# Other forms for the unread products ahead of the first head's maxima

## The chip, the cores and the metric

The kernel runs on one core of one Trainium2 chip. The metric is the time of one execution in device microseconds (us); the kernel before takes 967.83 us, the median of three runs (967.53 to 968.13).

## What is computed

Attention with a hash mask for 4 x 8 heads of 768 positions and 64 dimensions, and then a two-layer network on its result:

```python
q_bucket = np.sum(((q @ proj) > 0) * powers, -1)   # 6 bits; k_bucket likewise
scores = where(q_bucket[..., None] == k_bucket[..., None, :], scale * q @ k.T, -1e9)
attn = exp(scores - max(scores)); attn = attn / (sum(attn) + 1e-9)
x = (attn @ v) as [3072, 512]
h = x @ w_in                                        # 512 -> 2048
g = where(h >= 1, h, where(h <= -1, 0, (h + 1)**2 / 4))
return g @ w_out                                    # 2048 -> 512
```

## The kernel before, in words

All is float32. Where float32 accuracy is needed from single-pass products, an operand is split into a high part, rounded to the type float32r ("split form"), and the rest. The 32 heads are worked off in units of 128 keys x 384 queries: two products make the scores (lines 421 and 422), ScalarE takes the exponential, and three products gather the values (lines 454, 456, 458). The row maxima of a head are computed a few heads ahead by products of their own (line 343) that VectorE reduces (line 350). The network runs after that and between. Instructions of an engine run in the order in which the program writes them; a table of tasks per unit sets that order from the first unit on, and plain statements set it before.

The change touches only the start, which is written out by hand for pair 0:

- `keep_busy` (line 475) is one product whose result nobody reads. It multiplies `idle`, a 128 x 256 tile of zeros in float32r, by its first 128 columns, into a scratch half of a PSUM bank. It stands in four places: 14 times at the start, 5 times after the first head's bit products, once after each of the six score products of `max_first`, and 4 times later into another bank.
- `first_mm` (line 238) makes the hash bits of a head from two products for each half of the positions; ScalarE copies part of it (line 242), VectorE compares (line 247), and ScalarE and VectorE write the scaled bits (lines 254 and 256) into the tile that the score products read.
- `max_first` (line 495) computes the first half of the first head's maxima: six score products of 384 columns, each with an unread product after it and a VectorE maximum (line 498). Four PSUM tiles are taken in turn.
- After that come the second head's bit products (line 238 again), the next two score products (line 343), whose maxima VectorE takes at line 350, and three small products that turn the maxima into a row (line 274).
- `max_tr` (line 396) is the one place before where a float32 transposition runs on TensorE; line 398 does the same in split form as a product with the identity.

The order of the start is:

Of the kernel before, what the change touches and what calls it, by code (L numbers as in the profile page):

```python
# [11 lines left out]
F32 = mybir.dt.float32  # L12
# [8 lines left out]
B, H, S, D = 4, 8, 768, 64  # L21
NB = 6
P = 128
# [88 lines left out]
def attention(ctx, tc, wst, T1, T2, qk, v, pj, cv, x_d, s_d, e_d, tasks, shared):  # L112
    nc = tc.nc
# [10 lines left out]
    def half_bank(hf):  # L124
        return ps_f.tile([P, 512], F32, name=f"half{hf}")
# [8 lines left out]
    ident = const.tile([P, P], F32, name="ident")  # L134
# [3 lines left out]
    idle = const.tile([P, 2 * P], F32R, name="idle")  # L138
# [60 lines left out]
    def ones_row(h, eng):  # L199
        eng.memset(T2[0][32:33, 1, h].bitcast(F32), 1.0)  # L200
# [43 lines left out]
    def first_cmp(h, hf):  # L244
        sl = slice(hf * HS, (hf + 1) * HS)
        neg = neg_first[h]
        nc.vector.tensor_tensor(out=neg[:, sl], in0=neg_first[h, hf][0:40, 0:HS], in1=neg[:, sl], op=ALU.is_gt)
# [70 lines left out]
    def first_half(hd, a, b):  # L318
        return obank[1][:, 448 + hd * NJ + a:448 + hd * NJ + b] if in_bank(hd, a) else nmp(hd)[:, a:b]
# [6 lines left out]
    def nmp(hd):  # L326

        if hd not in nms:
            nms[hd] = small.tile([P, 2 * NJ], F32, name="nm")
        return nms[hd]  # L330
# [139 lines left out]

    scratch = half_bank(0)

    def keep_busy(ps=scratch):

        nc.tensor.matmul(out=ps[:, 0:2 * P], lhsT=idle[:, 0:P], rhs=idle, start=True, stop=True)  # L475

    def weights_pair(part):

# [9 lines left out]
    def max_first():  # L488

        t2 = T2[0]  # L490
        nm = first_half(0, 0, NJ), nmp(0)[:, NJ:2 * NJ]
        for hf in range(2):
            for i in range(NJ // 2):
                sm = ps_s.tile([P, 512], F32, name="s")
                nc.tensor.matmul(out=sm[:, 0:HS], lhsT=t2[:, 0, 0, i * P:(i + 1) * P],
                                 rhs=t2[:, 1, 0, hf * HS:(hf + 1) * HS], start=True, stop=True)
                keep_busy()
                nc.vector.tensor_reduce(out=nm[hf][:, i:i + 1], in_=sm[:, 0:HS], axis=AX.X,
                                        op=ALU.max, negate=True)

# [25 lines left out]
    nc.vector.memset(idle.bitcast(F32), 0.0)  # L526
    nc.vector.memset(pw.bitcast(F32), 0.0)
    nc.vector.memset(T2[0][0:64, 0].bitcast(F32), 0.0)
    for _ in range(14):
        keep_busy()  # L530
    make_identity(nc, ident)
    nc.gpsimd.tensor_copy(out=ident_r, in_=ident)
    for t in nrow:
# [15 lines left out]
    for hf in range(2):  # L549
        first_mm(0, hf, obank[hf])  # L550
    ones_row(0, nc.gpsimd)
    for _ in range(5):
        keep_busy()
    first_cmp(0, 0)
    first_scale(0, 0, nc.vector, 0)
    first_scale(0, 1, nc.scalar, 0)
# [5 lines left out]
    prep_first(1, first[1][:, 0], nc.gpsimd)  # L562
    place_first(1)
    max_first()
    row_clamp(0, 0, NJ // 2)
    for hf in range(2):
# [104 lines left out]
    for i in range(2 * NJ):  # L671
        n = 5 * 31 + 35 * i // 4
# [497 lines left out]
def lsh_attn_ffn(ctx: ExitStack, tc: tile.TileContext, qk, v, pj, cv, w_in, w_out, out):  # L1170
# [105 lines left out]
    for i in (2, 3):  # L1276
        at(NH * NU + 2 * i - 10, late[i + NFT - NW1][0])
    attention(actx, tc, wst, T1, T2, qk, v, pj, cv, x_d, s_d, e_d, tasks, attn)
    actx.close()

# [78 lines left out]
```

## Time and profile before

| what | us |
|---|---|
| median of the runs | 967.83 |
| the profiled execution: span from the first to the last instruction | 965.5 |
| what lies around the span, by the median | 2.3 |
| TensorE (PE) busy in the span | 957.1 |
| VectorE (DVE), ScalarE (ACT), GpSimd (POOL) busy | 752.7, 679.8, 322.7 |

The profiled execution has no time of its own beside its span. An engine's time is how long at least one of its instructions was on it; products are pipelined, so the duration of one is longer than its step to the next, and what a row of several tells is the distance of the starts. PEld is the loading of weights, which runs beside the product before it.

### The profile page before, as it was taken

The page shows a single profiled execution, that of the slowest core. Times are in us where ns is not written, and L with a number is a line of the kernel's source. Part 1 is how long each engine was busy: PE and PEld are TensorE (multiplying, and loading weights), DVE is VectorE, ACT ScalarE, POOL GpSimd, SP SyncE. Part 2 cuts the span into 40 slices and gives each one's busy share as a digit, 9 for nine tenths or more (in the row PEclk, how much of TensorE's full clock was granted, in tenths as well). Part 3 has the DMA queues.
Part 4 walks back from the last instruction along what each step waited for, and adds up shares of the span by engine and source line. Part 5 has one row for each costly group of instructions (what it writes and reads, how often), then busy time and mean ns, then how long its engine had stood idle before and what let it go on. Part 6 is the DMA issues. An engine that isn't in the chain of part 4 may idle for free.

```text
span 965.5 us, 15605 instructions
## 1 busy us (share of the span) xinstructions
PE 957.1 (99%) x5050; PEld 889.9 (92%) x5050; DVE 752.7 (78%) x1341; ACT 679.8 (70%) x1481; POOL 322.7 (33%) x435
## 2 busy tenths in 40 slices
PE   8999999999999999999999999999999999999998
PEld 7899999999999999999989998888998899888996
DVE  8878889888888889885987787787866777655554
ACT  7889999999999999987655465555564545544444
POOL 8867776666667776476000000000000000000000
PEclk9999999999999999999999999999999999999999
DMA  5776666666766666536691669966468554454431
GB/s 163 189 178 181 164 169 174 183 180 198 202 180 188 158 174 167 148 107 170 186 344 44 200 214 310 308 216 184 120 186 215 156 175 120 147 150 119 121 88 65
DMA packets 95112, 167.55 MB, mean 174 GB/s; under 512 B 13956, under 2 KB 51960, under 8 KB 95032
## 3 DMA queue, kind: packets, MB, share of 16 engines
q1 hardware_dynamic: 94768, 166.53, 60.1%
q8 instruction: 40, 0.66, 0.3%
q14 instruction: 40, 0.33, 0.1%
q10 hardware_dynamic: 264, 0.03, 0.0%
HBM read 106.13 MB, written 33.87 MB: 145 GB/s over the span
## 4 chain that ended last, share of the span: by engine, by line
PE 97%; DVE 2%; ACT 1%; issue 0%; DVEq 0%
PE y L893 27%; PE h L1125 18%; PE h L1030 7%; PE s L421 7%; PE o L458 7%; PE o L456 7%; PE o L454 7%; PE s L422 7%; PE smax L343 6%; PE o L219 2%; PE half L343 1%; DVE nm L350 0%; PE half L475 0%; DVE nm L323 0%; PE s L398 0%
## 5 line engine op out<-in xcount | busy, mean ns | idle before, releaser
L430 ACT ACTIVATE ph<-s 128x384 fp32r<-128x384 f32 x380 | 189.8, 500 | 32.1 <-PE s L422 26.1
L360 DVE TENSOR_REDUCE nm<-smax 128x1 f32<-128x768 f32 x168 | 159.9, 952 | 17.5 <-PE smax L343 17.5
L39 DVE TENSOR_TENSOR pl<-s,ph 128x384 fp32r<-128x384 f32 x256 | 137.9, 550 | 26.9 <-ACT s L435 25.6
L39 POOL TENSOR_TENSOR pl<-pf,ph 128x384 fp32r<-128x384 f32 x128 | 129.8, 1014 | 84.3 <-ACT pf L435 79.4
L858 DVE SCALAR_TENSOR_TENSOR t<-t 128x384 f32<-128x384 f32 x128 | 71.3, 557 | 106.7 <-ACT z L853 106.5
L421 PE MATMUL s<-t 128*128 128x384 f32 x384 | 130.5, 340 | 0.0
L454 PE MATMUL o<-ph,va 128*128 128x386 f32 x384 | 130.0, 339 | 0.0
L456 PE MATMUL o<-ph,vb 128*128 128x386 f32 x384 | 130.0, 338 | 0.0
L458 PE MATMUL o<-pl,va 128*128 128x386 f32 x384 | 130.0, 338 | 0.0
L422 PE MATMUL s<-t 128*128 128x384 f32 x384 | 129.4, 337 | 0.0
L435 ACT ACTIVATE s<-s 128x384 f32<-128x384 f32 x252 | 126.2, 501 | 0.0
L893 PE MATMUL y<-t,ghi 128*128 128x512 f32 x384 | 124.6, 395 | 0.0
L852 ACT ACTIVATE t<-h,mh 128x384 f32<-128x384 f32 x56 | 32.5, 581 | 83.7 <-PE h L1030 44.1
L343 PE MATMUL smax<-t 128*128 128x384 f32 x336 | 87.6, 342 | 0.4 <-DVE nm L360 0.3
L863 ACT CAST ghi<-z 128x384 fp32r<-128x384 f32 x129 | 65.2, 505 | 30.1 <-DVE z L859 26.3
L853 ACT ACTIVATE z<-t,m 128x384 f32<-128x384 f32 x128 | 79.0, 617 | 4.2
L893 PEld LDWEIGHTS y<-t,ghi 128*128 128x128 f32 x384 | 71.3, 188 | 11.0 <-ACT ghi L863 0.3
L1125 PE MATMUL h<-wbig,t 128*128 128x384 f32 x399 | 81.4, 336 | 0.0
L852 ACT ACTIVATE t<-wsq,mh 128x384 f32<-128x384 f32 x48 | 29.6, 617 | 67.0 <-DVE wsq L1138 40.8
L1125 PEld LDWEIGHTS h<-wbig,t 128*128 128x128 f32 x399 | 71.6, 188 | 5.2
L893 PE MATMUL y<-t,glo 128*128 128x512 f32 x192 | 76.0, 396 | 0.0
L893 PE MATMUL y<-woh,glo 128*128 128x512 f32 x192 | 75.7, 394 | 0.2
(206 smaller groups left out, 2104.2 us busy)
## 6 DMA issues: line engine op xcount, KB each, us to landing
t<-wc SPq DMA_DIRECT2D x92, 256.0 KB
t<-t SPq DMA_DIRECT2D x60, 384.0 KB
wraw<-wc SPq DMA_DIRECT2D x76, 256.0 KB
raw<-in_qk_dram SPq DMA_DIRECT2D x14, 768.0 KB
wraw<-in_w_in_dram SPq DMA_DIRECT2D x16, 512.0 KB
wraw<-in_w_out_dram SPq DMA_DIRECT2D x16, 512.0 KB
t<-ed SPq DMA_DIRECT2D x36, 192.0 KB
xd<-xs SPq DMA_DIRECT2D x32, 192.5 KB
```

Of the source, the lines that this page charges most:

```text
L39: eng.tensor_tensor(out=out, in0=a, in1=b, op=ALU.subtract)
L343: nc.tensor.matmul(out=ps[:, 0:HS], lhsT=t2[:, 0, h, i * P:(i + 1) * P], rhs=t2[:, 1, h, hf * HS:(hf + 1) * HS], start=True, stop=True)
L360: nc.vector.tensor_reduce(out=nmp(hd)[:, i:i + 1], in_=smax[hd][:, :, 0:HS], axis=AX.XY, op=ALU.max, negate=True)
L421: nc.tensor.matmul(out=ps[:, 0:HS], lhsT=t1[:, 1, h, ks], rhs=t1[:, 0, h, sl], start=True, stop=False)
L422: nc.tensor.matmul(out=ps[:, 0:HS], lhsT=t2[:, 1, h, ks], rhs=t2[:, 0, h, sl], start=False, stop=True)
L430: nc.scalar.activation(out=ph[:, 0:HS], in_=ps[:, 0:HS], func=AF.Exp, scale=SCALE)
L435: nc.scalar.activation(out=pf, in_=ps[:, 0:HS], func=AF.Exp, scale=SCALE)
L454: nc.tensor.matmul(out=o, lhsT=wa, rhs=ph, start=(jj == 0), stop=False)
L456: nc.tensor.matmul(out=o, lhsT=wb, rhs=ph, start=False, stop=False)
L458: nc.tensor.matmul(out=o, lhsT=wa, rhs=pl, start=False, stop=(jj == NJ - 1))
L893: nc.tensor.matmul(out=ys[c][m], lhsT=g_[:, m * P:(m + 1) * P], rhs=w, start=(first and k == 0), stop=(last and k == 2))
L1125: nc.tensor.matmul(out=ps, lhsT=w[:, cs], rhs=x, start=(n == 0 and s not in (2, 3, 6)), stop=(n == 5), skip_group_check=True)
```

## The change

`keep_busy` gets a form and a count. Form 0 is the old product. Form 1 is a plain float32 product of 66 columns, form 2 a split-form product of 130 columns, form 3 a split-form product of 66 columns, and the last is a float32 transposition of 128 columns. The weights have 128 columns in every form, taken from the first and second half of `idle` in turn. Results are unread as before.

```diff
+    idle_f = idle.bitcast(F32)
+
+    def keep_busy(ps=scratch, form=0, n=1):
+
+        for i in range(n):
+            ks = slice(i % 2 * P, (i % 2 + 1) * P)
+            if form == 0:
+                nc.tensor.matmul(out=ps[:, 0:2 * P], lhsT=idle[:, 0:P], rhs=idle, start=True, stop=True)
+            elif form == 1:
+                nc.tensor.matmul(out=ps[:, 0:D + 2], lhsT=idle_f[:, ks], rhs=idle_f[:, 0:D + 2], start=True, stop=True)
+            elif form == 2:
+                nc.tensor.matmul(out=ps[:, 0:P + 2], lhsT=idle[:, ks], rhs=idle[:, 0:P + 2], start=True, stop=True)
+            elif form == 3:
+                nc.tensor.matmul(out=ps[:, 0:D + 2], lhsT=idle[:, ks], rhs=idle[:, 0:D + 2], start=True, stop=True)
+            else:
+                nc.tensor.transpose(out=ps[:, 0:P], in_=idle_f[:, ks], identity=ident)
...
-                keep_busy()
+                keep_busy(form=(0, 1, 2, 3, 4, 1)[hf * 3 + i], n=(1, 3, 4, 4, 3, 3)[hf * 3 + i])
...
-    for _ in range(14):
-        keep_busy()
+    for form, n in ((0, 2), (1, 5), (2, 4), (3, 4), (0, 3)):
+        keep_busy(form=form, n=n)
...
-    for _ in range(5):
-        keep_busy()
+    for form, n in ((0, 2), (1, 4), (2, 4), (3, 2)):
+        keep_busy(form=form, n=n)
```

On TensorE, at the start of the program: the first set, ahead of the first head's four bit products (into the tiles `o_137` and `o_138`); `half_169` is the scratch.

```order
-L475 MATMUL half_169<-idle 128x256 x14
+L480 MATMUL half_169<-idle 128x256 x2
+L482 MATMUL half_169<-idle 128x66 x5
+L484 MATMUL half_169<-idle 128x130 x4
+L486 MATMUL half_169<-idle 128x66 x4
+L480 MATMUL half_169<-idle 128x256 x3
 L238 MATMUL o_137<-t_0_77,pw 128x384
```

Fourteen calls have become eighteen, five of them plain float (L482); the bit products follow as before.

On TensorE, from the second set to the second head's bit products, in the changed program (the six `L508` products are the first head's scores):

```order
L480 MATMUL half_169<-idle 128x256 x2
L482 MATMUL half_169<-idle 128x66 x4
L484 MATMUL half_169<-idle 128x130 x4
L486 MATMUL half_169<-idle 128x66 x2
L508 MATMUL s<-t_0_77 128x384
L480 MATMUL half_169<-idle 128x256
L508 MATMUL s<-t_0_77 128x384
L482 MATMUL half_169<-idle 128x66 x3
L508 MATMUL s<-t_0_77 128x384
L484 MATMUL half_169<-idle 128x130 x4
L508 MATMUL s<-t_0_77 128x384
L486 MATMUL half_169<-idle 128x66 x4
```

Before, five wide products stood ahead of the first score and one after each; now there are twelve, and then one, three, four and four.

On TensorE, the end of that stretch in the changed program:

```order
L508 MATMUL s<-t_0_77 128x384
L488 MATMUL half_169<-ident,idle 128x128 x3
L508 MATMUL s<-t_0_77 128x384
L482 MATMUL half_169<-idle 128x66 x3
L238 MATMUL s<-t_0_77,pw 128x384
```

Three transpositions and three plain-float products stand where one wide product stood each time, ahead of the second head's bit products. The rows count calls. The built program holds 5088 products and 5088 weight loads where the one before holds 5050 of each; 23 calls were added, so the 15 plain-float calls (5, 4, 3 and 3) make up the other 15, as two loads and two products each. VectorE, ScalarE, GpSimd and the DMA queues keep their instructions and their order.

## Rows read from the trace of the kernel before

**Rows 1.** The page: the span, the first engine's busy time, share and count, and the chain that ended last by engine.

```profile
span 965.5 us, 15605 instructions
PE 957.1 (99%) x5050; PEld 889.9 (92%) x5050; DVE 752.7 (78%) x1341; ACT 679.8 (70%) x1481; POOL 322.7 (33%) x435
PE 97%; DVE 2%; ACT 1%; issue 0%; DVEq 0%
```

**Rows 2.** Busy time by stretch: the stretch, its length, busy us and instructions of each engine, the granted TensorE clock, the DMA share and GB/s.

```profile
0.00:20.00 20.00, 17.13 (x85) 14.33 (x86) 17.39 (x42) 15.15 (x32) 15.53 (x48) 1.00 0.59 168
20.00:40.00 20.00, 19.16 (x105) 16.71 (x104) 17.04 (x37) 16.20 (x39) 18.59 (x26) 1.00 0.62 156
40.00:60.00 20.00, 19.13 (x101) 16.87 (x100) 17.48 (x34) 15.82 (x37) 14.33 (x20) 1.00 0.63 165
60.00:80.00 20.00, 20.00 (x115) 19.58 (x114) 16.65 (x26) 17.51 (x43) 12.28 (x16) 1.00 0.74 194
```

**Rows 3.** The chain of work that ended last, in order of time, in the first 13 us: start, us, what.

```profile
1.27 3.36 PE half L475 x14
4.63 1.66 PE o L238 x4
...
6.82 0.71 ACT t L254
...
8.79 0.57 DVE o L498
...
10.01 1.40 DVE nm L498 x3
```

**Rows 4.** TensorE in order of time from the first unread product to the score products at line 343: start, us to the end of the last of the row, line, output and inputs, count, and the wait before with its releaser.

```profile
1.27 3.36 PE L475 MATMUL half<-idle 128*128 128x256 f32 x14 [1.27 <-DVE idle L526]
4.57 1.70 PE L238 MATMUL o<-t,pw 128*128 128x384 f32 x4
6.07 0.81 PE L475 MATMUL half<-idle 128*128 128x256 f32 x5
7.66 0.41 PE L495 MATMUL s<-t 128*128 128x384 f32 x1 [0.78 <-ACT t L254]
...
8.02 0.34 PE L495 MATMUL s<-t 128*128 128x384 f32 x1
8.20 0.28 PE L475 MATMUL half<-idle 128*128 128x256 f32 x1
8.32 0.34 PE L495 MATMUL s<-t 128*128 128x384 f32 x1
...
8.77 0.44 PE L495 MATMUL s<-t 128*128 128x384 f32 x1
...
9.17 0.34 PE L495 MATMUL s<-t 128*128 128x384 f32 x1
...
9.46 0.38 PE L495 MATMUL s<-t 128*128 128x384 f32 x1
...
10.16 0.98 PE L238 MATMUL s<-t,pw 128*128 128x384 f32 x4 [0.20 <-DVE o L498]
10.97 0.51 PE L343 MATMUL half<-t 128*128 128x384 f32 x2
```

**Rows 5.** TensorE again, in narrow windows before 6 us: two unread products and the last one alone, and the second and third of the bit products.

```profile
4.00 0.63 PE L475 MATMUL half<-idle 128*128 128x256 f32 x2
...
4.21 0.41 PE L475 MATMUL half<-idle 128*128 128x256 f32 x1
...
5.05 0.84 PE L238 MATMUL o<-t,pw 128*128 128x384 f32 x2
```

**Rows 6.** Weight loads in order of time, two that follow an idle array before 6 us and two after: start, us, line.

```profile
5.58 0.29 PEld L238 LDWEIGHTS o<-t,pw 128*128 128x128 f32 x1 [0.20 <-DVE t L39]
5.75 0.34 PEld L475 LDWEIGHTS half<-idle 128*128 128x128 f32 x1
...
7.63 0.19 PEld L495 LDWEIGHTS s<-t 128*128 128x128 f32 x1 [0.96 <-POOL t L186]
7.74 0.19 PEld L475 LDWEIGHTS half<-idle 128*128 128x128 f32 x1
```

**Rows 7.** VectorE in order of time: the six first maxima and the first of the next.

```profile
8.11 1.91 DVE L498 TENSOR_REDUCE o<-s 128x1 f32<-128x384 f32 x3
9.92 1.48 DVE L498 TENSOR_REDUCE nm<-s 128x1 f32<-128x384 f32 x3
...
11.84 0.57 DVE L350 TENSOR_REDUCE o<-half 128x1 f32<-128x384 f32 x1
```

**Rows 8.** ScalarE in order of time: the copy out of the first bit products and the scaled bits.

```profile
5.61 0.49 ACT L242 ACTIVATE xs<-o 40x384 f32<-40x384 f32 x1 [0.75 <-PE o L238]
...
6.82 0.71 ACT L254 ACTIVATE t<-xs,cvd 8x384 fp32r<-8x384 f32 x1
```

**Rows 9.** The products of two lines (shortest, median and longest in ns, first and last start): line 396, the float32 transposition, and line 398, the same in split form; then the first of line 396 in order of time and the stretch around it.

```profile
L396 PE MATMUL o<-ident,nm x2: 272/274/275, 28.5 to 35.6; 128*12 128x128 f32 x2
...
L398 PE MATMUL s<-ident_r,nmr x29: 220/225/231, 57.6 to 431.3; 128*12 128x128 f32 x29
...
28.46 0.27 PE L396 MATMUL o<-ident,nm 128*12 128x128 f32 x1
...
28.00:30.00 2.00, 1.93 (x10) 1.39 (x9) 1.89 (x5) 0.77 (x3) 2.00 (x3) 1.00 0.02 7
```

More of the change, by code (lines that the diff above doesn't have):

```diff
@@ L471, in attention @@
     scratch = half_bank(0)
-    def keep_busy(ps=scratch):
-        nc.tensor.matmul(out=ps[:, 0:2 * P], lhsT=idle[:, 0:P], rhs=idle, start=True, stop=True)
+    idle_f = idle.bitcast(F32)
[12 more added lines that the diff above has]
+                nc.tensor.transpose(out=ps[:, 0:P], in_=idle_f[:, ks], identity=ident)
     def weights_pair(part):
```

## The prediction

> **What bounds the kernel now.** I read the page first: TensorE is busy 957.1 of 965.5 us and the chain that ended last is TensorE for 97% [rows 1]. So whatever delays TensorE's steady stream delays the end, and nothing in that stream is touched. The table by stage then shows where TensorE is not full: 17.13 of the first 20 us, 19.16 and 19.13 of the next two twenties, and 20.00 of 20.00 from 60 us on [rows 2]. The change lies in the first 11 us, so I read the chain in order of time there: it goes from the unread products (1.27) to the first head's bit products (4.63), over ScalarE (6.82) to the first score, and from there through VectorE's six maxima (8.79, 10.01) [rows 3] to the next maxima at 11.84 [rows 7]. TensorE is on the path before 6 us, waits until 7.66, and runs ahead of VectorE after that. The reader is to see that this stage has two places that pay for longer filling (before 4.57, and from 9.5 to 11.3) and one that forgives it (6.9 to 7.66).
>
> **Prices of one unread product.** Here the rows on spacing matter, not the durations, since records overlap. A 256-column product steps by 0.21 us at first (4.00 to 4.21) [rows 5]. That is TensorE's lower level, 1.2 GHz, by the spacing; the granted-clock column reads 1.00 for the first 20 us [rows 2], so it does not cover this stretch. The five at 6.07 take 0.81 with a last one of 0.28, so they step by 0.13 [rows 4]: the clock rose at about 6.2.
> A short product is not bound by its columns: 66 or 130 columns take half of 256 or less. It is bound by its weight load, which has 128 columns in every form. Two loads of which the first is exposed start 0.17 apart at the lower level (5.58, 5.75) and 0.11 apart at the upper (7.63, 7.74) [rows 6]. I take these two as the price of a short product; the bounds are 0.11 and 0.21 at the lower level (a load that ignores the clock, a full 256-column step) and 0.11 to 0.13 at the upper.
> Plain float: the built program has 38 more products and 38 more loads than before for 23 more calls, so each of the 15 plain-float calls is two loads and two products, and costs 0.34 and 0.22. If each product streams its 66 columns twice, 132 columns stay shorter than the load. The Trainium skill (FP8 and Floating Point Precision, section TensorE Precision Notes) gives true FP32 four passes through the array; with a load for each pass a call would cost 0.68 and 0.44, and the sum would come near 972.5 us. No row here shows it, and I stay with the two loads that the program holds.
> Float transposition: the one in the trace takes 274 ns against 225 for the same 128 columns in split form [rows 9], 0.05 more, so its columns take about 0.11, as long as a load: 0.11 each.
>
> **First set (14 products become 18 calls).** Before: 14 x 0.21 = 2.94, the last columns end at 4.21 + 0.21 = 4.42 [rows 5], and the bit product's load at 4.57 puts its columns at about 4.74, after VectorE's bit weights. Now: 5 x 0.21 for the wide ones, 18 x 0.17 for 10 plain-float and 8 short split halves, 4.11 in all, 1.17 more. The columns end at 5.59, with the next load hidden beneath them, so the bit products are late by 5.59 - 4.74 = 0.85. They still step by 0.32 at the lower level (5.05 for two, 0.84) [rows 5], so the chain ScalarE copy (5.61), scale (6.82) [rows 8], first score (7.66) is late by the same 0.85: 8.51. Bounds: 18 short ones at 0.11 give 3.03, 0.09 over before, which fits into the idle time ahead of 4.74: no delay; at 0.21 they give 4.83, so 1.6.
>
> **Second set (5 become 12).** 2 x 0.12 + 14 x 0.11 = 1.78 in place of 0.6. The fourth bit product now starts near 6.4, the set ends near 8.35, and the first score is not wanted before 8.51. Hidden by the wait of 0.78 that stood before 7.66; with that cover gone every microsecond more would be late. Cost 0.
>
> **Between the maxima (6 become 18).** Measured from the first score product. Before: scores at 0, 0.36, 0.66, 1.11, 1.51, 1.80, the second head's bit products at 2.50, the next score pair at 3.31 [rows 4], VectorE's maximum on it at 4.18 [rows 7]. A score steps 0.18 (8.02 to 8.20 is 384 columns), then come the loads: scores now at 0, 0.36, 1.20 (six loads), 1.82 (four), 2.44 (four), 2.95 (three transpositions), and after six more loads the bit products at 3.79. Four of these at 0.17 put the score pair at 4.47, its end at 4.81, and the maximum at 4.85, 0.67 late. VectorE's six maxima are hardly touched: the last score ends at 3.29 and the last maximum began at 10.85, which is 3.19, so 0.1 to 0.15 late [rows 7], and that is inside the 0.67. What forgives is that the pair's product stood ready about 0.5 before VectorE came to it (10.97 + 0.34 against 11.84). Bounds: 0.5 with the transpositions at half price, 0.9 with 0.13 for each load.
>
> **Sum.** 0.85 + 0 + 0.67 = 1.5 us. DVE, ACT, POOL and SP keep their instructions and order; no DMA is added or moved. GpSimd's casts follow the bit products and move with them, ahead of what waits for them. The profiled execution's span is 965.5, so 967.0 now; the median of the runs, 967.83, stands 2.3 above it for what lies around the span, so **969.3 us**. That is 0.16% more; about 0.2%, 1.9 us, is what a measurement of this kernel can tell from no change.
>
> **Rivals.**
> 1. The clock rises later. The unread products stand there while nothing else runs, and the thin forms stream columns for a smaller part of each step. If TensorE stayed at 1.2 GHz through the second set, that set would cost 2 x 0.21 + 14 x 0.17 = 2.8, start near 6.9 and end at 9.7, so the first score is another 1.2 late: 2.7 in all, 970.5. If it lasted through the maxima as well, scores would step 0.32 and loads 0.17, the maximum after them comes 3.7 late in place of 0.67: 5.7 in all, 973.5. For it: the rise at 6.2 came after 14 wide products. Against: there is no pause in either set, and the waits of TensorE at 7.66 and 10.16 [rows 4] did not bring the clock down. It decides once it adds 0.4 us. The Trainium skill (TensorE: Matmul & The Clock Gate, Part 4) says that transposition does not count as busy for the clock gate; by that three transpositions near 11 us would help the clock fall. The stretch around the transposition at 28.46 reads 1.00 [rows 9], but that is a single one.
> 2. Most of it is hidden. Short loads at the lower level might step by 0.11, so the first set costs nothing, and a delay may be taken up by the 1.7 us that TensorE still idles from 20 to 60 us [rows 2]. Then only 0.2 to 0.7 is left: 968.0 to 968.5. Against: where the chain leaves TensorE in rows 3 it is for VectorE and ScalarE, which are late by the same amount.
> 3. Each load takes a full step of 0.21 at the lower level. Then the first set is 1.6 late, the sum 2.3, 970.1.
> 4. Faster: the bit products, coming later, meet the higher clock. It would save at most their 4 x 0.15, 0.6, and that is part of the delay they already have. No mechanism here gives 1.9 us.
>
> **How the numbers follow.** Forecast with loads at 0.17 and 0.11: 0.50, its own range 968.9 to 969.7. Hidden: 0.18. Full steps: 0.12. Clock later: 0.18. Faster 0.02. The first two are within 0.2%, 0.68; full steps (970.1) and the later clock are beyond it, 0.30. The range takes in most of hidden (from 968.2) and full steps and the shorter of the two clock cases (971.0), and leaves out about 0.15.
>
> **What would show it.** In the changed trace: short products stepping 0.17 before 6 us and 0.11 after; two loads for each plain-float call; the first bit product's columns near 5.6; no more than 0.1 us of wait before the first score at 8.5; the second head's bit products about 3.8 after that; the maximum now at 11.84 near 13.4; everything after shifted by 1.5. Wrong: 384-column products still 0.32 apart after 7 us (rival 1), or the first score at 7.7 to 8.0 (rival 2).

## The result and the profile after

The changed kernel takes 971.32 us (median of six runs, 971.03 to 976.37) against 967.98 for the kernel before (six runs, 967.53 to 968.62): over all runs a ratio of 1.0051, interval 1.0028 to 1.0074, and 1.0035 between the two medians. Four of the six runs stand at 971.0 to 971.5 and two at 976.37, nothing between; the interval is wide because it holds both. The forecast was 969.3, range 968.2 to 971.0: no change that can be measured. By the medians the time is 3.3 us, 0.35%, above before, and above the range.

The page of the profiled execution, one of the shorter kind (971.15 us, span 969.0), against [rows 1]:

```profile
span 969.0 us, 15681 instructions
PE 961.6 (99%) x5088; PEld 895.3 (92%) x5088; DVE 752.3 (78%) x1341; ACT 679.9 (70%) x1481; POOL 322.7 (33%) x435
```

TensorE is busy 4.5 us longer, but that is unread work; what counts is where it delays the rest. TensorE in order of time, same columns as [rows 4]:

```profile
1.27 0.80 PE L480 MATMUL half<-idle 128*128 128x256 f32 x2 [1.27 <-DVE idle L539]
1.86 2.23 PE L482 MATMUL half<-idle 128*128 128x66 f32 x10
3.85 1.09 PE L484 MATMUL half<-idle 128*128 128x130 f32 x4
4.74 1.00 PE L486 MATMUL half<-idle 128*128 128x66 f32 x4
5.56 0.99 PE L480 MATMUL half<-idle 128*128 128x256 f32 x3
6.34 1.48 PE L238 MATMUL o<-t,pw 128*128 128x384 f32 x4
7.62 0.60 PE L480 MATMUL half<-idle 128*128 128x256 f32 x2
8.05 1.01 PE L482 MATMUL half<-idle 128*128 128x66 f32 x8
...
9.54 0.42 PE L508 MATMUL s<-t 128*128 128x384 f32 x1
...
10.09 0.78 PE L482 MATMUL half<-idle 128*128 128x66 f32 x6
...
13.27 0.94 PE L238 MATMUL s<-t,pw 128*128 128x384 f32 x4
14.05 0.51 PE L343 MATMUL half<-t 128*128 128x384 f32 x2
```

The weight loads of the first set in order of time, same columns as [rows 6]:

```profile
1.65 2.25 PEld L482 LDWEIGHTS half<-idle 128*128 128x128 f32 x10
3.78 0.97 PEld L484 LDWEIGHTS half<-idle 128*128 128x128 f32 x4
4.63 0.97 PEld L486 LDWEIGHTS half<-idle 128*128 128x128 f32 x4
5.49 0.76 PEld L480 LDWEIGHTS half<-idle 128*128 128x128 f32 x3
```

Three readings. The ten loads of the plain-float calls take from 1.65 to 3.78, 0.213 each and not 0.17, and the two groups of four behind them 0.21 each as well, with 130 and with 66 columns; the bit products start at 6.34. Those four still step by 0.32 (1.48 less a last one of 0.52, over three), and the two wide ones after them by 0.21, so the clock came up at about 8.05 and not at 6.2; eight products after that take 1.01, 0.11 each. And the 0.78 of waiting before the first score [rows 4] is gone: that score starts at 9.54, 1.88 late.

The chain of work that ended last (start, us, what) now runs through the second set, which [rows 3] did not:

```profile
6.54 1.28 PE o L238 x4
7.82 0.40 PE half L480 x2
8.22 0.84 PE half L482 x8
9.06 0.45 PE half L484 x4
9.51 0.19 PE half L486 x2
9.70 0.26 PE s L508
...
14.21 0.19 PE half L343
14.43 0.58 DVE o L350
```

VectorE in order of time, against [rows 7]: the next maximum now waits for its product.

```profile
9.99 1.91 DVE L511 TENSOR_REDUCE o<-s 128x1 f32<-128x384 f32 x3 [0.41 <-PE s L508]
11.81 1.63 DVE L511 TENSOR_REDUCE nm<-s 128x1 f32<-128x384 f32 x3
...
14.43 0.57 DVE L350 TENSOR_REDUCE o<-half 128x1 f32<-128x384 f32 x1 [0.65 <-PE half L343]
```

That maximum stood at 11.84; it is 2.59 late.

### The profile page after: what moved, and what is told of

The parts are those of the page before. It is cut to its first block, busy times and chain, and to the rows that moved or that the text cites. A ratio compares the mean times of both kernels' runs of the same rounds, so it can differ in the third digit from the quotient of the medians.

```text
span 969.0 us, 15681 instructions
## 1 busy us (share of the span) xinstructions
PE 961.6 (99%) x5088; PEld 895.3 (92%) x5088; DVE 752.3 (78%) x1341; ACT 679.9 (70%) x1481; POOL 322.7 (33%) x435
## 4 chain that ended last, share of the span: by engine, by line
PE 95%; DMA 2%; DVE 1%; ACT 1%; issue 0%; SPq 0%; POOL 0%; ACTq 0%; POOLq 0%
PE y L906 27%; PE h L1138 18%; PE h L1043 7%; PE s L421 7%; PE s L422 7%; PE o L454 7%; PE o L458 7%; PE o L456 7%; PE smax L343 6%; PE o L219 2%; DMA raw<-in_qk_dram 1%; PE half L343 1%; DMA t<-te 0%; PE half L482 0%; DMA vraw<-in_v_dram 0%
```

## The experiments

Two theories. **A, length**: back-to-back loads at the lower level of the clock (1.2 GHz, against 2.4 GHz at the upper) step 0.213, so the changed first set is just 23 steps long in place of 14, and that and the loads between the maxima are the cost. **B, clock**: the thin products (66 or 130 columns, against 256 in the wide ones) leave the clock low for longer, so that the following sets pay the lower level's price; the runs at 976.4 are those in which it stays low through the maxima. The granted-clock column reads 1.00 in all these stretches; the rises below are read from the spacing of products, and the last section has them from the record of the clock.

All edits are against the changed kernel. `W1`, `W2`, `WL` stand for the old first set, the old second set and the old single product between the maxima:

```diff
-    for form, n in ((0, 2), (1, 5), (2, 4), (3, 4), (0, 3)):
+    for form, n in ((0, 14),):                                # W1
-    for form, n in ((0, 2), (1, 4), (2, 4), (3, 2)):
+    for form, n in ((0, 5),):                                 # W2
-                keep_busy(form=(0, 1, 2, 3, 4, 1)[hf * 3 + i], n=(1, 3, 4, 4, 3, 3)[hf * 3 + i])
+                keep_busy()                                   # WL
```

| run | first set | second set | maxima | median us | before, same chip | ratio (interval) |
|---|---|---|---|---|---|---|
| e1 | changed | W2 | WL | 969.70 | 967.88 | 1.0018 (1.0009 to 1.0026) |
| e2 | W1 | changed | WL | 968.26 | 967.88 | 1.0004 (0.9995 to 1.0013) |
| e3 | W1 | W2 | changed | 968.52 | 967.88 | 1.0007 (0.9998 to 1.0016) |
| e4 | 14 thin | W2 | WL | 968.36 | 967.88 | 1.0003 (0.9994 to 1.0012) |
| e5 | 23 wide | W2 | WL | 968.41 | 967.58 | 1.0009 (1.0000 to 1.0017) |
| e6 | 23 wide | changed | changed | 969.61 | 967.58 | 1.0021 (1.0012 to 1.0030) |
| e7 | 23 thin | changed | changed | 976.57 | 967.58 | 1.0091 (1.0076 to 1.0107) |
| e8 | changed | changed | changed | 971.05 | 967.58 | 1.0036 (1.0024 to 1.0049) |
| e9 | W1 | changed | changed | 968.94 | 967.80 | 1.0012 (1.0003 to 1.0020) |
| e10 | 14, mixed forms | changed | changed | 974.81 | 967.80 | 1.0061 (1.0044 to 1.0079) |

**The three parts alone (e1, e2, e3).** Edits: e1 takes `W2` and `WL`, e2 `W1` and `WL`, e3 `W1` and `W2`.

> Only the first set has the new forms (18 calls, 23 products); the second set and the products between the maxima are as before. Theory A (back-to-back loads at the lower clock step 0.213 us each, so the set is simply 23 steps long in place of 14): the bit products' columns start near 6.34 in place of 4.74, 1.6 us late, the first score 1.6 late (near 9.25), and the time is 1.6 to 2.2 us over before, with the clock's rise of no weight since the wait for the first score covers it. Theory B (thin forms keep the clock down, and that is what costs): the clock rises near 8 us or later, and the time is 2.5 us or more over before. My forecast's own step (0.17) would give 0.85.

> Only the second set has the new forms (12 calls, 16 products); the rest as before. Theory A: the clock rises where it did (near 6.2), 16 products at 0.11 end near 7.8 in place of 6.7, the first score waits 0.1 to 0.2 us more than before, and the time is 0 to 0.3 us over before. Theory B: thin forms after the rise bring the clock down again; products of 384 columns stand 0.32 apart somewhere between 8 and 13 us, and the time is over 1 us over before in some or all executions.

> Only the products between the maxima have the new forms (18 calls, 24 products in place of 6); the rest as before. Theory A: from the first score to VectorE's maximum on the next pair 4.85 to 4.9 us in place of 4.18, so 0.7 us over before, in all executions. Theory B (thin products and transpositions let the clock fall): products of 384 columns at 0.32 apart after the maxima, and executions that are 3 to 6 us over before, as two of the six of the whole change were.

Measured: 1.8, 0.4 and 0.6 us over before; only the first is clear of noise, as the intervals of e2 and e3 take in no change. e1 lies where A put it, and its traced bit products start at 6.34 with the first score at 9.27, as A said. But the clock in it came up only at about 11: its first scores step by 0.53 (9.94, 10.47, 11.00). That cost little there, since one wide product and a score are 0.53 and VectorE's maxima last 0.55 each; the maximum on the next pair is at 13.70, 1.86 late. e2's first score is at 8.00, 0.34 late, a little over A's figure, though its clock was up near 6.5. In e3 the maximum is at 12.43, 4.89 after its first score at 7.54, where before it was 4.18: the 0.7 forecast. None of the 33 runs is above 970. The three add up to 2.8. The whole at 3.3 to 3.5 cannot be told from that sum within these intervals; the whole at 8.4, in two of its runs, is more than the sum.

**Thin, but no longer (e4).**

```diff
-    for form, n in ((0, 2), (1, 5), (2, 4), (3, 4), (0, 3)):
+    for form, n in ((3, 14),):
```

and `W2`, `WL`.

> The first set is 14 split-form products of 66 columns in place of 14 of 256; everything else as before. It separates the length of the set from the thinness of its products. Theory A: each steps 0.213 by its load, the set is as long as before, the bit products start where they did (4.6 to 4.7), and the time is within 0.3 us of before. My forecast's step of 0.17 would end the set 0.6 us earlier, with no effect on the time, as the bit weights come at 4.52. Theory B: the clock rises later than 6.2 us, so that scores and unread products run at the lower level after 7.66, and the time is 1 to 4 us over before.

TensorE of e4 in order of time:

```profile
1.27 3.20 PE L486 MATMUL half<-idle 128*128 128x66 f32 x14 [1.27 <-DVE idle L539]
4.55 1.70 PE L238 MATMUL o<-t,pw 128*128 128x384 f32 x4
6.05 1.27 PE L480 MATMUL half<-idle 128*128 128x256 f32 x5
7.64 0.66 PE L508 MATMUL s<-t 128*128 128x384 f32 x1 [0.32 <-ACT t L254]
8.10 0.41 PE L480 MATMUL half<-idle 128*128 128x256 f32 x1
8.31 0.52 PE L508 MATMUL s<-t 128*128 128x384 f32 x1
...
10.98 1.09 PE L238 MATMUL s<-t,pw 128*128 128x384 f32 x4
11.91 0.51 PE L343 MATMUL half<-t 128*128 128x384 f32 x2
```

Both theories are half right. Fourteen products of 66 columns take nearly as long as fourteen of 256 (3.20 here, 3.36 in [rows 4]), so the step is the load's 0.21. And the clock, which came up near 6.2 after wide ones, stays low until about 11.4: the second set's five wide ones take 1.27 against 0.81, the scores step by 0.53 and more. Yet the time is only 0.5 over before, which its interval does not tell from no change, where B expected 1 to 4: with one unread product between two scores VectorE covers it.

**Length without thinness, and the whole with either first set (e5, e6, e7, e8).** First sets:

```diff
+    for form, n in ((0, 23),):   # e5 (with W2, WL) and e6
+    for form, n in ((3, 23),):   # e7
```

e8 is the changed kernel again.

> The first set is 23 split-form products of 256 columns, as many as the changed set has products; everything else as before. It has the length of the changed set without its thinness. Theory A (length alone): the clock rises at 5 to 7 us as before, the last products of the set and the bit products run at 0.12 and 0.17 after that, the first score is 1.1 to 1.6 us late, and the time is 1.1 to 1.6 us over before, less than the 1.8 of the changed first set alone. Theory B (the thin products of the first set add to it by a late clock): the difference to the changed first set alone is 0.2 to 0.7 us.

> The whole change, but with 23 split-form products of 256 columns as the first set. Theory A (what costs is the length of the first set and the loads between the maxima): 3.0 to 3.4 us over before in all executions, like the change. Theory B (the two executions of the change at 976.4 are ones in which the clock stayed at the lower level through all of the start): no execution above 972, since the wide first set raises the clock near 6 us; the time is 2.0 to 2.6 us over before, below the change.

> The whole change, but with 23 split-form products of 66 columns as the first set: the same 23 steps of 0.213, all thin. Theory A: 3.0 to 3.5 us over before, as the change. Theory B: the clock stays at the lower level through the second set and the maxima in most executions; worked out at 0.213 for each load and 0.32 for each 384-column product, the first score is 3.4 us late and VectorE's maximum on the next pair 8.1, so most executions stand near 976, 8 us over before.

> The change itself once more, for the shares of its two times and a second trace. Theory A: one time, 971.0 to 971.6, and the two executions at 976.4 were disturbances that do not come back. Theory B: both times come back, 971 in some two thirds of the executions and 976.4 in some third, by where the clock's rise falls (near 8 us, or after the maxima); if the trace is of the second kind, its 384-column products stand 0.32 apart from 6 to beyond 14 us, and the maximum on the next pair comes near 20.

e5 costs 0.8, with an interval that touches no change, less than A's bound, and 1.0 less than the mixed set of equal count, more than B's 0.2 to 0.7. In its trace 23 wide ones take only 4.35 and the bit products start at 5.46 and take 0.85 for four: the clock came up while the set still ran. That is not so each time. TensorE of e6, with the same first set:

```profile
1.27 5.28 PE L480 MATMUL half<-idle 128*128 128x256 f32 x23 [1.27 <-DVE idle L539]
6.34 1.26 PE L238 MATMUL o<-t,pw 128*128 128x384 f32 x4
...
7.67 1.00 PE L482 MATMUL half<-idle 128*128 128x66 f32 x8
```

Here the bit products start as late as in the change, and the clock comes up during them. What 9 wide steps more delay the bit products by thus differs from one execution to another with the rise of the clock: 0.7 us in one trace and 1.6 in the other. e6, the whole change after a wide first set, has all eleven runs between 969.0 and 970.6, 2.0 over before by the median: where B put it, and below A's 3.0. e7 has its four at 975.2 to 977.0. The sets after the first are the same in both; 7 us lie between a wide and a thin first set of 23 products. TensorE of e7:

```profile
1.27 5.11 PE L486 MATMUL half<-idle 128*128 128x66 f32 x23 [1.27 <-DVE idle L539]
6.20 1.63 PE L238 MATMUL o<-t,pw 128*128 128x384 f32 x4
7.62 0.63 PE L480 MATMUL half<-idle 128*128 128x256 f32 x2
8.05 1.81 PE L482 MATMUL half<-idle 128*128 128x66 f32 x8
...
10.89 0.67 PE L508 MATMUL s<-t 128*128 128x384 f32 x1
...
11.89 1.38 PE L482 MATMUL half<-idle 128*128 128x66 f32 x6
13.02 0.67 PE L508 MATMUL s<-t 128*128 128x384 f32 x1
...
17.93 1.63 PE L238 MATMUL s<-t,pw 128*128 128x384 f32 x4
19.36 0.84 PE L343 MATMUL half<-t 128*128 128x384 f32 x2
```

The eight products at 8.05 take 1.81 where the change's took 1.01, the six at 11.89 take 1.38 where they took 0.78, and the score products still step by 0.32 at 19.36. VectorE's maximum follows at 19.91, 8.1 after 11.84. B worked out 8.1 from the lower level's steps, but with the first score 3.4 late, and it is 3.2 late (10.89): that the total fits to the tenth is in part luck. By its end e7's span is 9.0 longer, as the lower level lasts on past that maximum. Now VectorE waits for every score:

```profile
13.73 0.57 DVE L511 TENSOR_REDUCE o<-s 128x1 f32<-128x384 f32 x1 [0.90 <-PE s L508]
14.90 0.56 DVE L511 TENSOR_REDUCE nm<-s 128x1 f32<-128x384 f32 x1 [0.61 <-PE s L508]
...
19.91 0.57 DVE L350 TENSOR_REDUCE o<-half 128x1 f32<-128x384 f32 x1 [1.98 <-PE half L343]
```

e8 has five runs, all at 970.6 to 971.1, as A had it and not B: the time of 976 stands in two of the change's eleven runs in all, and its share stays unknown; its first score is at 9.95 and its maximum at 14.83, 2.99 late, with a span of 968.5, 3.0 longer.

**The old first set, and the new one cut to the old length (e9, e10).** e9 takes `W1`; e10:

```diff
-    for form, n in ((0, 2), (1, 5), (2, 4), (3, 4), (0, 3)):
+    for form, n in ((0, 2), (1, 2), (2, 3), (3, 2), (0, 3)):
```

> The whole change, but with the first set as before (14 split-form products of 256 columns). Theory A (the pieces add up): the 0.4 of the second set alone and the 0.6 of the maxima alone, so 0.9 to 1.2 us over before. Theory B (clock): the same, since the wide first set has the clock up near 6 us; no execution above 970. If the thin products after it brought the clock down again, some executions would stand at 973 to 976.

> The whole change, with the first set cut to 14 products of the same mixed forms (2 wide, 2 plain-float calls, 3 and 2 short ones, 3 wide), so that it is as long as before at 0.213 a step. Theory A (length is what costs): the bit products start where they did before, and only the second set and the maxima are left: 0.9 to 1.2 us over before. Theory B (the mixed set leaves the clock low when the second set begins, whose 14 loads then cost 0.213 each in place of 0.11): the second set ends near 9.4 if the clock is not up before, the first score is up to 1.8 us late, and the time is 1.5 to 3 us over before, or near 976 where the clock stays down through the maxima.

e9 is 1.1 over before, about the sum of e2 and e3, no run above 970. e10 parts the two theories. Its first set is as long as before, so by A it should equal e9; five of its six runs stand at 974.5 to 975.1 and one at 969.28. Its trace (974.51 us):

```profile
4.57 1.71 PE L238 MATMUL o<-t,pw 128*128 128x384 f32 x4
6.08 0.63 PE L480 MATMUL half<-idle 128*128 128x256 f32 x2
6.50 1.81 PE L482 MATMUL half<-idle 128*128 128x66 f32 x8
...
9.34 0.67 PE L508 MATMUL s<-t 128*128 128x384 f32 x1
...
16.38 1.63 PE L238 MATMUL s<-t,pw 128*128 128x384 f32 x4
17.81 0.76 PE L343 MATMUL half<-t 128*128 128x384 f32 x2
18.40 0.34 PE L274 MATMUL o<-ident_r,nrow 128*33 128x128 f32 x3
```

The bit products start on time at 4.57, and all that follows runs at the lower level up to about 18.3. One kernel at two times, 969.3 and 974.8, is the change's 971 and 976 over again, 1.6 to 1.8 us earlier, which is the length that was cut.

So the cost of the change is both: a first set 9 steps longer, which moves everything by 1.6 us while the clock is low; and a late clock, which turns the 16 and 24 products after it from 0.11 into 0.21 each, in part of the second set (0.3 and 0.7 us) in the two traces of the runs near 971, and, as inferred from e7 and e10, through the maxima in those at 976. Where the clock is up early the same 9 steps cost less: 0.8 in e5 over before, 0.9 between e9 and e6. No run points to a version that beats the kernel before.

## Why the prediction was wrong

- **The first set: 0.85 forecast, 1.60 measured.** The failed step is the price of 0.17 for a short product at the lower level. It came from a load into an idle array followed by a second one [rows 6]; in a queue the loads step by 0.213 (1.65 to 3.78 for ten). The bound of 0.21 and its 1.6 us stood in the text as rival 3, with a chance of 0.12. The same rows had a hint that I passed over: the load behind another lasts 0.34, the exposed one 0.29, so that a pair need not tell the distance in a queue.
- **The second set: 0 forecast, 0.28 in one trace and 0.68 in the other.** The price of 0.11 at the upper level was right, but the clock was not up: it rose 0.4 us into the set in one trace and about 1.3 in the other. The step took the rise at 6.2 from the trace of before as if it belonged to the time and not to the products that had run. It also had less cover than it says: by its own rows the fourth bit product starts at 5.05 + 2 x 0.32 + 0.85 = 6.54 and not near 6.4, so the set ends near 8.5, with nothing to spare before 8.51. In e2 the rise came 0.4 us into the set too, at 6.5, and the first score was 0.34 late; in e9 it came before the set, and the first score was on time (7.64).
- **Between the maxima: 0.67 forecast, 0.71 and 0.70 measured**, and 0.7 in e3. The mechanism was right too: VectorE's last of the six maxima began 3.35 after the first score (11.81 + 1.63 - 0.55 - 9.54) in place of 3.19, and the product for the next maximum lost its lead.
- **The sum carries to the end.** In e8 the maximum is 2.99 late and the span 3.0 longer. In the first trace 2.59 became 3.5 by the end, 0.3 of it near 62 us and most of the rest between 200 and 500 us. The kernel before itself spreads over 1.1 us here, so I take that for spread; its cause is not shown.
- **The rivals.** Rival 1 was the right mechanism for the late clock, with 5.7 us for its long form; I left out of that price that the first set would be 1.6 and not 0.85 late and that the short products step 0.21 at the lower level. With both the price is 8.1 for the maximum, where e7 has 8.07. Treating rivals 1 and 3 as alternatives was the second error: neither excludes the other (e10 has the late clock without the length, e6 the length without the late clock), so their costs come together. As delays of the maximum they make 2.6 in one trace and 3.0 in the other (1.6, 0.3 or 0.7, 0.7), which by the forecast's sum is 970.4 and 970.8, still inside its range. The shorter runs of the change, up to 971.5, lie somewhat above that, as the first trace does by the growth after its maximum; the two at 976.37 are, by inference, the long form of rival 1, which the range left out.
- **A side estimate.** Four loads for each plain-float call were said to bring the sum near 972.5; by the forecast's own terms it is 973.0 (969.3 + 5 x 0.34 + 4 x 0.22 - 0.16 + 6 x 0.22). Nothing rests on it, as each call has two loads.
- Its argument against rival 1, that there is no pause in either set, fell: e4 has hardly any before 7.3 us, and the clock stayed low to 11.4.

What stays open: no execution of the change at 976.4 was caught in a trace, only those of e7 and e10; that those two are the same is inferred from the same two times in e10. Why some executions of one kernel get the clock and others don't was not tried, nor were transpositions apart from the other forms.

## What to carry to other kernels

A short unread product is not a cheap one: with a full weight load in front it costs the load (here 0.21 us at the lower level, as much as 256 columns), and the plain-float form costs two. Products that are there to bring the clock up must be judged by what the work behind them runs at, and the place to look is not their own stretch but the first queue of many small products after it, which pays for every one at the lower level (here 0.21 us in place of 0.11). Rivals that do not exclude each other are to be added, not weighed against each other.

## What the runs showed of the hardware

A load of 128 columns steps by 0.11 us at the upper level and, queued, by 0.213 at the lower; 66, 130 and 256 columns behind it make next to no difference at the lower level: behind 23 products the bit products start at 6.20 (all of 66 columns, e7), 6.34 (mixed, the change) and 6.34 (all of 256, e6). The Trainium skill (TensorE: Matmul & The Clock Gate, section LDWEIGHTS) gives a load as its columns over 1.2, which is 107 ns for 128: the trace agrees at the upper level and shows twice that at the lower.

A plain-float product of 66 columns runs as two loads and two products, 0.43 us at the lower level (ten loads from 1.65 to 3.78) and 0.22 at the upper (two steps of 0.11). The Trainium skill (FP8 and Floating Point Precision, section TensorE Precision Notes) speaks of four passes; the trace shows two records for each call, and no cost beyond their two loads.

Each trace keeps a record of the granted clock. It begins with the rise to the upper level, and nothing stands ahead of it; the column reads 1.00 there all the same. One trace of each run, in us from the start of the span; the first unread product starts at 1.27 in all:

| first set | the clock rises at |
|---|---|
| 14 wide | 6.19 (before), 6.51 (e2), 5.42 (e3), 4.24 (e9) |
| 23 wide | 4.33 (e5), 7.20 (e6) |
| 23, mixed | 8.05 (the change), 8.91 (e8), 11.21 (e1) |
| 14, mixed | 18.34 (e10) |
| 14 of 66 columns | 11.46 (e4) |
| 23 of 66 columns | 21.94 (e7) |

In none of them does TensorE wait for more than 0.4 us at a time between its first product and the rise. One and the same first set has it about 3 us apart, so a single trace does not tell the time of a rise; but all six rises behind a wide set lie before 7.3, and all six behind a mixed or thin one after 8.0.
